# Loading and scanning the first 256 tokens whole instead of in two pieces, in a gated recurrence followed by a cosine feed-forward

## The chip, the cores and the metric

The kernel runs on one core of one Trainium2 chip. The metric is the device time of one execution in microseconds (us). One execution was also profiled, and its trace is what the lines below come from; a trace's span is about 1.8 us shorter than the time of the same execution. All executions quoted here were fast. A single core has no second die to compare with, so "fast" says only that the execution was within 1.5% of the fastest.

## The reference

```python
def _attn_ref(x, f_logit, lower_bound):          # x: 4 x 6080 x 256
    sig = 1.0 / (1.0 + np.exp(-f_logit))
    f = lower_bound + (1.0 - lower_bound) * sig
    i = 1.0 - f
    for t in range(S):
        h = f[:, t] * h + i[:, t] * x[:, t]
        y[:, t] = h
    return y

def _moe_ref(x, w_in, w_out):                    # w_in 256 x 2048, w_out 2048 x 256
    h = x @ w_in
    g = h * np.cos(h)
    return g @ w_out
```

The recurrence's output is the feed-forward's input. All is float32 outside; the kernel multiplies in float16.

## The kernel before

Tokens go through in chunks: seven of 256, then 512 each. For a chunk, ScalarE makes the gate, VectorE or GpSimd the term u, TensorE (chunks 0 to 3) or a transposing DMA (chunk 4 and later) turns both so that channels lie on partitions, VectorE scans, and the result yb feeds `mm1` (with w_in), a cosine, a product T, and `moe2` (with w_out). w_in comes in four quarters of its columns. Quarters 0 and 1 come as float32 ("raw") over SyncE's queue and are rounded by engines; quarters 2 and 3, all of w_out and the inputs of chunk 2 come over GpSimd's queue ("GpSimd's stream" below). `keep_warm` issues matmuls on zeros ("junk") that keep TensorE's clock up while it waits. The loads of chunk 3 and later wait until w_out's last quarter is in place.

```python
    emit_load(0, 0, P)                     # z and x of tokens 0..127
    load_win(0, cast=False)                # raw quarter 0, SyncE's queue
    emit_load(0, P, HALF)                  # tokens 128..255
    load_win(1, cast=False)
    emit_load(1)
    ...
    round_win(0, 0, nc.gpsimd.tensor_copy)
    load_win(2)                            # GpSimd's queue from here
    load_win(3)
    round_win(1, 0, nc.gpsimd.tensor_copy)
    load_wout(0); load_wout(1)
    emit_load(2, q=nc.gpsimd)
    load_wout(2)
    w_in_place = load_wout(3)              # chunk 3's loads wait for this one
    ...
    for c in range(3, NC):                 # woven between the matmul groups
        ...                                # chunk 4 on: less_one, pool_term (GpSimd),
        ...                                # turn (DMA transpose), forget (GpSimd), recur, cast
```

## Time and profile before

| | before |
|---|---|
| time, median of the three executions | 681.64 us (680.82 to 681.65) |
| TensorE busy | 670.9 of 679.7 us (99%) |
| VectorE, ScalarE, GpSimd busy | 583.2, 518.2, 315.1 us |
| TensorE's clock | 1.000 |

At a share of 99% the end moves when TensorE's few idle stretches move. They lie in the first 37 us of the trace ("the head"), with one of 0.35 us at 99 us. The profile's lines are shown in the prediction.

### The profile page before, as it was taken

To read this page: it belongs to the slowest core of one execution; us is meant where nothing else is said; L and a number is where in the kernel's file an instruction comes from. 1 tells how busy PE (TensorE), PEld (TensorE's weight loads), DVE (VectorE), ACT (ScalarE), POOL (GpSimd) and SP (SyncE) were. 2 spreads that over 40 slices of the span, in tenths; PEclk is the share of its full clock that TensorE was granted. 3 is DMA by queue.
4 is the path that set the end of the run, shared out by engine and by line. 5 is a ranking of instruction groups with operands and counts; after the bars stand their busy time and mean duration, and the time that the engine had idled before them with its cause. 6 is when DMAs were issued, how large, how long until landed. Compare 5 with 4: busy or idle time off the path is not lost.

```text
span 679.7 us, 12405 instructions
## 1 busy us (share of the span) xinstructions
PE 670.9 (99%) x4826; PEld 494.6 (73%) x4826; DVE 583.2 (86%) x507; ACT 518.2 (76%) x587; POOL 315.1 (46%) x442
## 2 busy tenths in 40 slices
PE   7999999999999999999999999999999999999998
PEld 4899987777777777777777777777777777777776
DVE  5898998888888888888888888888888888888884
ACT  6887788777877788777877788777877788777762
POOL 5478454445454445445454445445454445445300
DMA  8799756656667556764776556764686566632301
GB/s 205 198 259 225 201 157 154 169 140 124 160 188 150 124 140 175 167 139 125 159 189 150 124 142 175 158 148 124 163 185 149 124 144 178 162 76 63 94 32 62
DMA packets 173290, 101.99 MB, mean 150 GB/s; under 512 B 99120, under 2 KB 172080, under 8 KB 173232
## 3 DMA queue, kind: packets, MB, share of 16 engines
q1 hardware_dynamic: 171680, 99.11, 59.5%
q0 software_dynamic: 1280, 2.10, 1.7%
q8 instruction: 37, 0.61, 0.4%
q14 instruction: 21, 0.17, 0.1%
q10 hardware_dynamic: 272, 0.00, 0.0%
HBM read 54.00 MB, written 24.90 MB: 116 GB/s over the span
## 4 chain that ended last, share of the span: by engine, by line
PE 88%; DVE 4%; DMA 3%; issue 2%; ACT 1%; POOL 1%; SPq 0%; ACTq 0%; DVEq 0%; POOLq 0%
PE pb L312 45%; PE pa L271 43%; DVE T L286 3%; DVE ya L218 2%; DMA wo<-in_moe_w_out_dram 1%; DMA wir<-in_moe_w_in_dram 1%; ACT cs L280 1%; DMA zt<-in_f_logit_dram 1%; ACT ig L122 0%; SPq L82 0%; POOL wo L106 0%; POOL u L163 0%; ACT ig L150 0%; POOL xt L82 0%; POOL zt L82 0%
## 5 line engine op out<-in xcount | busy, mean ns | idle before, releaser
L286 DVE TENSOR_TENSOR T<-pa,cs 128x1024 f16<-128x1024 f32 x380 | 449.1, 1212 | 81.5 <-ACT cs L280 81.1
L280 ACT ACTIVATE cs<-pa 128x1024 f32<-128x1024 f32 x380 | 389.3, 1028 | 144.0 <-PE pa L271 132.4
L312 PE MATMUL pb<-wo,T 128*128 128x256 f16 x3040 | 393.0, 273 | 0.6 <-DMA wo<-in_moe_w_out_dram 0.6
L271 PE MATMUL pa<-yb,wi 128*128 128x512 f16 (+2 forms) x1736 | 390.3, 353 | 2.9 <-DMA wi<-in_moe_w_in_dram 1.4
L312 PEld LDWEIGHTS <-T 128*128 128x128 f16 x3040 | 297.3, 98 | 100.1 <-issue 1.0
L271 PEld LDWEIGHTS <-wi 128*128 128x128 f16 x1736 | 193.3, 114 | 75.5 <-issue 2.0
L232 POOL TENSOR_SCALAR yb<-ya,hc 128x512 f16<-128x512 f32 (+1 forms) x97 | 65.8, 679 | 187.5 <-DVE ya L218 186.6
L218 DVE TENSOR_TENSOR_SCAN ya<-ff,ya,ut 128x512 f32<-128x512 f32 (+4 forms) x94 | 131.3, 1398 | 0.6 <-POOL ff L199 0.6
L163 POOL TENSOR_TENSOR u<-ig,xt 128x256 f16<-128x256 f32 x182 | 130.3, 748 | 0.0
L161 POOL CAST ih<-ig 128x1024 f16<-128x1024 f32 (+1 forms) x47 | 47.5, 1010 | 137.1 <-ACT ig L150 135.1
L199 POOL TENSOR_SCALAR ff<-it,hp 128x512 f32<-128x512 f16 (+1 forms) x94 | 62.9, 683 | 1.5 <-DMA it<-ih 1.5
L320 ACT COPY osb<-pb 128x512 f32<-128x512 f32 x93 | 53.8, 579 | 0.7 <-PE pb L312 0.7
L122 ACT ACTIVATE ig<-zt 128x1024 f32<-128x1024 f32 (+2 forms) x52 | 51.7, 994 | 2.0 <-DMA zt<-in_f_logit_dram 1.9
L150 ACT ACTIVATE ig<-ig 128x1024 f32<-128x1024 f32 x44 | 46.9, 1066 | 0.0
L339 PE MATMUL warm<-junk 128*128 128x512 f16 x15 | 5.7, 543 | 1.3 <-POOL junk L328 1.3
L218 DVE TENSOR_TENSOR_SCAN ya<-ff,ya,tp 128x256 f32<-128x256 f32 (+1 forms) x8 | 5.0, 665 | 1.3 <-ACT ff L196 1.3
L218 DVE TENSOR_TENSOR_SCAN ya<-ff,ut 128x320 f32<-128x320 f32 (+2 forms) x6 | 5.6, 928 | 0.0
L317 DVE COPY osb<-pb 128x256 f32<-128x256 f32 x4 | 1.7, 424 | 4.5 <-PE pb L312 4.5
L139 DVE SCALAR_TENSOR_TENSOR u<-ig,xt 128x512 f16<-128x512 f32 (+1 forms) x5 | 3.2, 645 | 2.5 <-DMA xt<-in_x_dram 1.7
L339 PEld LDWEIGHTS <-junk 128*128 128x128 f16 x18 | 2.1, 126 | 4.0 <-issue 2.2
L137 POOL TENSOR_SCALAR ih<-ig 128x512 f16<-128x512 f32 x2 | 1.7, 866 | 6.2 <-ACT ig L122 6.2
L99 POOL CAST wi<-wir 128x512 f16<-128x512 f32 x2 | 1.5, 748 | 4.9 <-DMA wir<-in_moe_w_in_dram 4.8
(29 smaller groups left out, 27.2 us busy)
## 6 DMA issues: line engine op xcount, KB each, us to landing
zt<-in_f_logit_dram SPq DMA_DIRECT2D x44, 512.0 KB, 5.1
xt<-in_x_dram SPq DMA_DIRECT2D x44, 512.0 KB, 6.0
out_dram<-osb SPq DMA_DIRECT2D x43, 512.0 KB, 3.4
out_dram<-osb SPq DMA_DIRECT2D x7, 256.0 KB, 5.1
zt<-in_f_logit_dram SPq DMA_DIRECT2D x5, 256.0 KB, 5.2
xt<-in_x_dram SPq DMA_DIRECT2D x5, 256.0 KB, 5.6
wir<-in_moe_w_in_dram SPq DMA_DIRECT2D x2, 512.0 KB, 5.4
wo<-in_moe_w_out_dram POOLq DMA_DIRECT2D x4, 256.0 KB, 7.1
```

Source lines behind the costliest of these rows:

```text
L122: nc.scalar.activation(ig[:, ks, :], zt[:, ks, :], AFT.Tanh, bias=0.0, scale=0.5)
L150: nc.scalar.activation(ig[:, ks, :], ig[:, ks, :], AFT.Identity, bias=-1.0, scale=1.0)
L161: nc.gpsimd.tensor_copy(by_half(ih), split(ig))
L163: nc.gpsimd.tensor_tensor(by_half(u)[:, k], split(ig)[:, k], split(xt)[:, k], AOP.mult)
L199: nc.gpsimd.tensor_scalar(f[:, a:b], igt[:, i, 0:b - a], hp[:, i:i + 1], 1.0, AOP.mult, AOP.add)
L218: nc.vector.tensor_tensor_scan(ya[:, p:q], f[:, p:q], ut[:, i, p - a:q - a], init, AOP.mult, AOP.add)
L232: nc.gpsimd.tensor_scalar(yb[:, a:b], held[f"ya{i}", c][:, a:b], hc[:, i:i + 1], 0.0, AOP.mult, AOP.add)
L271: nc.tensor.matmul(pa[c, g][:, jq, a:b], win_block(i, jt), held[f"yb{i}", c][:, first + a:first + b], start=(i == 0), stop=(i == ND - 1))
L280: nc.scalar.activation(cs[c, g], pa[c, g], AFT.Sin, bias=float(_HALF_PI), scale=1.0)
L286: nc.vector.tensor_tensor(T, pa[c, g], cs[c, g], AOP.mult)
L312: nc.tensor.matmul(ps[:, ts % 2, :], Tt[c, ts, jt], wo[:, jt, :], start=(jt == 0), stop=(jt == NJ - 1))
L320: nc.scalar.copy(osb[:, ts - 1:ts + 1, :], ps)
```

## The change

Its intent: the first chunk of 256 tokens runs through in one go, with half as many instructions, and GpSimd is spared one rounding so that it issues its transfers sooner.

```diff
-    emit_load(0, 0, P)
+    emit_load(0)
     load_win(0, cast=False)
-    emit_load(0, P, HALF)       # it stood between raw quarters 0 and 1
 ...
     round_win(0, 0, nc.gpsimd.tensor_copy)
     load_win(2)
     load_win(3)
-    round_win(1, 0, nc.gpsimd.tensor_copy)
     load_wout(0)
 ...
-    gate(0, 0, P); term(0, 0, P); turn(0, 0, P)
-    keep_warm(8)
-    forget(0, 0, P); settle(0, 0, P)
-    gate(0, P, HALF)
-    round_win(0, 1, nc.vector.tensor_copy)
-    term(0, P, HALF); turn(0, P, HALF); forget(0, P, HALF)
-    mm1(0, 0, 0, P)
-    settle(0, P, HALF)
-    keep_warm(3, 1)
-    round_win(1, 1, nc.vector.tensor_copy)
-    mm1(0, 0, P, HALF)
+    gate(0); term(0); turn(0)
+    keep_warm(6)
+    forget(0)
+    round_win(0, 1, nc.scalar.copy)
+    settle(0)
+    round_win(1, 0, nc.vector.tensor_copy)
+    round_win(1, 1, nc.vector.tensor_copy)
+    mm1(0, 0)
```

(The `hc`, `hp` and lower-bound lines and the split of chunk 0's PSUM tile are left out.)

More of the change, by code (lines that the diff above doesn't have):

```diff
@@ L168, in turn @@
         if c < NPE:
-            apart = c == 1
+            apart = c < 2
             got = [ppool.tile([P, 1 if apart else 2, ND, HALF], f16, tag="p2", bufs=2,
@@ L328, with keep_warm @@
     nc.gpsimd.memset(junk, 0.0)
-    def keep_warm(k, g=None):
-        if g is None:
-            ps = ppool.tile([P, CH], f32, tag="p1", bufs=3, name=f"warm{len(warm)}",
-                            padded_shape=[P, 2 * CH])
-            warm.append(ps)
-        else:
-            ps = room(0, g)[:, 0:CH // HALF, :].rearrange("p j n -> p (j n)")
+    def keep_warm(k):
+        ps = ppool.tile([P, CH], f32, tag="p1", bufs=3, name=f"warm{len(warm)}",
+                        padded_shape=[P, 2 * CH])
+        warm.append(ps)
         for _ in range(k):
@@ L368 @@
     nc.vector.tensor_copy(ident, ident32)
-    gate(0, 0, P)
-    term(0, 0, P)
+    gate(0)
+    term(0)
     nc.vector.tensor_scalar(hc, lb, 0.5, -0.5, AOP.mult, AOP.add)
     nc.vector.tensor_scalar(hp, lb, -0.5, 0.5, AOP.mult, AOP.add)
-    turn(0, 0, P)
-    keep_warm(8)
-    forget(0, 0, P)
-    settle(0, 0, P)
-    gate(0, P, HALF)
-    round_win(0, 1, nc.vector.tensor_copy)
-    term(0, P, HALF)
-    turn(0, P, HALF)
-    forget(0, P, HALF)
-    mm1(0, 0, 0, P)
-    settle(0, P, HALF)
-    keep_warm(3, 1)
+    turn(0)
+    keep_warm(6)
[3 more added lines that the diff above has]
+    round_win(1, 0, nc.vector.tensor_copy)
     round_win(1, 1, nc.vector.tensor_copy)
-    mm1(0, 0, P, HALF)
+    mm1(0, 0)
     gate(1)
```

## The prediction

> **What bounds the kernel now.** I read the page's shares first, then busy time in stretches, then TensorE's instructions in the first 22 us, then the chain that ended last.
>
> The windows view gives busy time by stretch (columns: stretch, its length, then busy us and count for PE, PEld, DVE, ACT, POOL, then clock, DMA share, GB/s).
>
> ```profile
> 8.00:10.00 2.00, 1.43 (x15) 0.86 (x13) 1.12 (x4) 1.20 (x4) 1.92 (x4) 1.00 0.98 249
> 20.00:22.00 2.00, 1.75 (x17) 1.51 (x18) 1.84 (x3) 1.56 (x3) 0.00 (x0) 1.00 0.12 26
> 38.00:660.00 622.00, 621.62 (x4430) 455.65 (x4428) 545.82 (x459) 483.65 (x537) 295.45 (x406) 1.00 0.62 151
> ```
>
> From 38 to 660 us TensorE is busy 621.62 of 622 us, at full clock. The change touches only instructions issued before about 12 us. So it can move the end only by moving the moment at which TensorE becomes continuously fed. That moment is found in TensorE's timeline (start, duration, engine, line, operands, count; in brackets the idle time before and what ended it).
>
> ```profile
> 9.81 1.68 PE L271 MATMUL pa<-yb,wi 128*128 128x128 f16 x16 [0.57 <-ACT yb L225]
> 11.34 0.39 PE L176 MATMUL tp<-ident,ih 128*128 128x128 f16 x4
> ...
> 12.08 1.06 PE L271 MATMUL pa<-yb,wi 128*128 128x256 f16 x8
> 14.49 2.04 PE L271 MATMUL pa<-yb,wi 128*128 128x256 f16 x16 [1.35 <-DMA wi<-in_moe_w_in_dram]
> ...
> 17.36 0.60 PE L312 MATMUL pb<-wo,T 128*128 128x256 f16 x4 [0.38 <-DMA wo<-in_moe_w_out_dram]
> ...
> 21.08 0.60 PE L312 MATMUL pb<-wo,T 128*128 128x256 f16 x4 [0.25 <-DMA wo<-in_moe_w_out_dram]
> ```
>
> The first chunk's own work (row at 9.81) is not the last limit. After it TensorE waits four times for weights: the trace has quarter 2 of w_in landing at 12.03 (row at 12.08), quarter 3 at 14.45, quarter 1 of w_out at 17.32 and quarter 3 of w_out at 21.04. After 21.08 it has one more gap, 0.48 us at 36.97. The chain of waits says where that one comes from (start, length, what):
>
> ```profile
> 3.11 5.97 DMA wir<-in_moe_w_in_dram
> 9.08 0.06 issue
> 9.14 0.61 POOL wi L99
> 9.75 1.29 POOL wo L106 x2
> 11.04 0.71 POOL zt L82
> 11.76 0.73 POOL xt L82
> 12.49 0.55 POOL wo L106
> 13.04 8.00 DMA wo<-in_moe_w_out_dram
> 21.04 0.02 issue
> 21.06 0.37 SPq L82
> ```
>
> Inputs of chunks 3 to 6 are held back until the last w_out quarter has landed (21.04), and the gap at 37 hangs on these inputs. Both late limits therefore start from one time, the landing of w_out's last quarter. At first sight the chain promises a gain: its second step is GpSimd waiting for raw quarter 1 and rounding it (0.61 us), which the change deletes. But its 8.00 us step is a queueing time. GpSimd issued that last transfer by 13.62, and the transfers landing in front of it came at 16.01, 17.32, 18.04, 18.75 and 19.79. From 10 to 20 us the windows give DMA shares of 1.10, 0.91, 1.08, 1.08 and 0.99. The 16 engines are full, so an earlier issue only makes the transfer wait longer. What counts is when this stream starts: its first packet is at about 9.0 us.
>
> **What the Trainium skill says.** "DMA: Bandwidth & Descriptors", section "Issuing engines are not separate DMA queues", says that transfers of all issuing engines end on the same 16 DMA engines and interleave. The trace agrees: packets of SyncE's and GpSimd's queues overlap between 9 and 10 us at a share of 0.98. "SBUF — State Buffer", section "Who interferes with whom", says that a two-port VectorE operation, copies and casts among them, and GpSimd lock each other out of a shared port pair. The trace fits: GpSimd's 128x512 cast took 0.89 us beside VectorE's cast at 6.58 and 0.61 us at 9.14 with no such cast beside it. "TensorE: Matmul & The Clock Gate", section "What's actually happening", says that about 3.4 us of activity releases a halved clock. The 128x512 warming matmuls start 427 ns apart up to 5.56 us and 216 ns apart from 5.96, which agrees.
>
> **The change, part by part.**
>
> Loads. z and x of chunk 0 become two 256 KB transfers instead of four of 128 KB. SyncE issues two fewer transfers, each about 0.48 us from one issue to the next, so quarter 1 is issued at about 2.13 instead of 3.11. Bytes are unchanged. What moves is the order: 256 KB of 1,024-byte packets now stand ahead of raw quarter 0. These packets took 46 ns each; 256 of them on 16 engines are 256 x 46 / 16 = 0.74 us. Quarter 0 was issued at 1.66 in both, so it lands about 0.65 us later, 6.53 to about 7.2 (I take off 0.1 because in the kernel before, pieces behind it already shared its tail). Quarter 1 has the same bytes ahead as before and lands at about 9.0 (9.08 before), at best a few tenths sooner.
>
> First scan. z lands at about 3.55. A tanh of 128x512 took 0.64 us (row of chunk 1), and the 1-tanh copy the same: ih is ready at 4.85. u (0.68 us) is ready at about 4.95, as x lands near 4.3. Eight transposes at 107 ns, still cold, end near 5.9, the first four near 5.45. Two forget factors at 0.42 us (0.84 for two, at 11.76) end at 6.5. Two scans at 0.69 us (1.38 for two, at 12.86) end near 7.4, and VectorE's yb near 7.7. ScalarE now rounds half of quarter 0 before its yb: 7.2 + 0.64 = 7.85, then yb 0.51 = 8.4. The first real matmul starts at about 8.4 against 7.99, but it is the whole chunk: eight steps of 109 ns end it at 9.3, where before its second half started at 9.81.
>
> Quarter 1. VectorE rounds both halves, 2 x 0.42 from 9.05: ready at 9.9, against 10.36. Its matmuls run from 9.9 to 10.8, against 10.4 to 11.5. The transposes of chunk 1 remain tied to u of chunk 1 near 11.6, since VectorE does 0.42 us more before it but starts the pair 0.9 us sooner. So TensorE is through with chunk 1's transposes at about 12.0 as before, and the 0.6 us won before that become waiting for quarter 2.
>
> GpSimd. It gains 0.61 us and its wait for quarter 1, but it starts 0.65 us later on quarter 0. Its cast is now beside ScalarE's and not VectorE's; I take 0.65 us instead of 0.89. So it starts issuing quarter 2 at 7.2 + 0.05 + 0.65 = 7.9 against 7.41, and the stream's first packet is at 9.0 + 0.45 = 9.45. By 9.0 SyncE's queue is nearly drained (62 packets of 1,024 bytes left, 0.18 us of 16 engines), so the delay mostly becomes idle DMA time. Of the 0.45 us I count 0.1 as returned, because in that stretch SyncE's packets have the engines alone. w_out's first transfer is then issued at about 7.9 + 1.65 = 9.55, close to the old 9.69 and far ahead of its turn.
>
> Sum: the last w_out quarter lands 0.35 us later, 21.4. Nothing after it absorbs this: TensorE's wait of 0.25 us becomes 0.6, and the loads that lead to the gap at 37 shift with it. 681.64 + 0.35 = 682.0; I add 0.1 for the lopsided risks below and predict 682.1.
>
> **The rivals.** (1) Quarter 0 lands no later, or GpSimd's issues decide. For it: the chain names GpSimd's second rounding. Against: the full DMA shares. Even if the landing came much sooner, TensorE's waits for weights after 14.49 are 0.38 + 0.25 = 0.63 us and other operands wait close behind; I would give this 681.2. (2) The slow start of w_in grows with the shift. Raw packets of 2,048 bytes took 185 to 257 ns at 3.5 to 4.5 us and 84 to 101 ns later; if that is a fixed time from first touch, quarter 0 slips the full 0.74, GpSimd's cast is again blocked (0.89), and the stream starts 0.8 us late: 682.4. (3) TensorE loses its clock. It has one pause more before the scans (4.3 to 5.0), two fewer warming matmuls then and three fewer later, and a wait from 10.8 to 11.2. At half clock the eight matmuls after quarter 2 cost 0.9 us more, but 1.35 us of waiting for quarter 3 covers them; only if it were still cold after 14.8 would up to some 1.5 us show: 683.5. I give this one in ten. (4) The early first matmul wins. It would need weights to be there; they are not, so its worth is zero.
>
> **Range and chances.** The three timed runs before span 680.82 to 681.65, a spread of 0.8 us, as large as the effect. With rivals at 681.2 and 682.4 and the rare 683.5, I take 681.2 to 683.0. A move of 2% is 13.6 us; the whole head up to 21 us has 21 us in it and neither version can gain or lose that much. Within 2%: 0.99.
>
> **What would show it.** Raw quarter 0 landing near 7.2; GpSimd's first issue near 7.9; first matmul near 8.4; quarter 2, 3 and last w_out landing each about 0.35 us later (12.4, 14.8, 21.4), with the wait before that last one grown to about 0.6. If w_out's last quarter lands at or before 21.0 while quarter 0 lands late, the argument that the stream's start decides is wrong. If matmuls after 12 us step by 213 ns, rival 3 is true.

## The result, and the profile after

The changed kernel took 683.51 us (683.28 to 683.55, four executions) beside 681.23 us (680.58 to 681.65) for the kernel before. The ratio is 1.0034, 95% interval 1.0016 to 1.0051. Ratios here are the mean time of one kernel's fast executions over that of the other's of the same rounds, so not quite the ratio of the medians that are quoted. The time lies outside the range of 681.2 to 683.0, though within 2% as forecast.

TensorE after, first 22 us (columns as in the prediction):

```profile
8.59 2.42 PE L271 MATMUL pa<-yb,wi 128*128 128x256 f16 x16 [1.30 <-ACT yb L225]
...
12.96 1.06 PE L271 MATMUL pa<-yb,wi 128*128 128x256 f16 x8 [0.82 <-DMA wi<-in_moe_w_in_dram]
14.84 3.41 PE L271 MATMUL pa<-yb,wi 128*128 128x256 f16 x16 [0.81 <-DMA wi<-in_moe_w_in_dram]
18.04 1.27 PE L312 MATMUL pb<-wo,T 128*128 128x256 f16 x8
```

The first real matmul came at 8.59, quarter 2's at 12.96 and quarter 3's at 14.84; 8.4, 12.4 and 14.8 were predicted. But the 16 matmuls at 14.84 took 3.41 us where before they took 2.04. The windows view tells why in its clock column (third from the right):

```profile
14.00:16.00 2.00, 1.19 (x8) 0.92 (x8) 2.00 (x3) 1.05 (x2) 0.48 (x1) 0.77 1.10 197
16.00:18.00 2.00, 2.00 (x11) 1.42 (x10) 0.65 (x2) 1.04 (x1) 0.00 (x0) 0.50 1.08 335
...
38.00:660.00 622.00, 620.36 (x4419) 453.33 (x4419) 544.44 (x458) 483.00 (x536) 295.73 (x407) 1.00 0.60 151
```

TensorE ran at half its clock from 15.1 to 18.5 us. That is the third rival, for which the prediction had 683.5 us, just what was measured, and it is tempting to stop here. Two readings say that the match is luck. Of the four executions two had a mean clock of 0.997 (this stretch) and two 1.000, and they took 683.51 and 683.55 against 683.51 and 683.28: the same. And the lateness of one and the same product T in the two traces does not stay where the slow clock put it:

| product T number | ends, before | ends, after | later by |
|---|---|---|---|
| 5th | 19.07 | 20.57 | 1.50 |
| 10th | 29.57 | 30.05 | 0.49 |
| 29th | 64.11 | 65.61 | 1.50 |
| last | 670.71 | 672.62 | 1.91 |

By 30 us TensorE had caught up to 0.49 us, since it no longer had to stand where it stood before. Then, near 61 us, 1.4 us were lost anew (TensorE's `moe2` matmuls are 0.49 us late at 60.4 us and 1.91 us late at 64.9 us), long after the last changed instruction. In the last windows line above TensorE's busy time is 620.36 instead of 621.62 of 622 us. Its timeline shows the place, before:

```profile
59.28 1.04 PE L312 MATMUL pb<-wo,T 128*128 128x256 f16 x8
60.15 1.23 PE L271 MATMUL pa<-yb,wi 128*128 128x256 f16 x8
```

and after:

```profile
59.77 1.04 PE L312 MATMUL pb<-wo,T 128*128 128x256 f16 x8
61.70 0.27 PE L271 MATMUL pa<-yb,wi 128*128 128x256 f16 x1 [0.90 <-POOL yb L232]
62.37 0.93 PE L271 MATMUL pa<-yb,wi 128*128 128x256 f16 x7 [0.40 <-POOL yb L232]
```

TensorE waits for GpSimd's yb of chunk 7. GpSimd's timeline before it, first in the kernel before:

```profile
51.18 0.93 POOL L232 TENSOR_SCALAR yb<-ya,hc 128x256 f16<-128x256 f32 x2
52.09 1.36 POOL L199 TENSOR_SCALAR ff<-it,hp 128x512 f32<-128x512 f16 x2
...
59.04 1.36 POOL L232 TENSOR_SCALAR yb<-ya,hc 128x512 f16<-128x512 f32 x2
```

and in the changed one:

```profile
51.79 0.93 POOL L232 TENSOR_SCALAR yb<-ya,hc 128x256 f16<-128x256 f32 x2
54.00 1.37 POOL L199 TENSOR_SCALAR ff<-it,hp 128x512 f32<-128x512 f16 x2 [1.28 <-DMA it<-ih]
...
60.96 1.36 POOL L232 TENSOR_SCALAR yb<-ya,hc 128x512 f16<-128x512 f32 x2
```

Before, GpSimd works from 45.7 to 60.4 us without a gap, and TensorE takes its last yb the moment it is ready: this feed had no slack that TensorE's busy share could show. After, GpSimd stands 1.28 us for the transpose of chunk 7. That transpose was issued 0.61 us later (48.29 against 47.68) but landed 2.07 us later (53.91 against 51.84). The trace records 16 completions of each such DMA, and the last of them is its landing: 51.69 to 51.84 for all 16 before; 52.53 to 52.62 for fifteen of them after, and 53.91 for the sixteenth.

What delayed one completion? The trace lists, beside data packets, packets of kind "instruction": blocks of 8 KB and 16 KB of the program itself, fetched while it runs. Before, 8 KB blocks were fetched at 42.7, 45.3 and 51.9 us; after, at 44.4, 52.05 and 52.94. One of these two now ends just before the first completion and the other begins between the fifteenth and the sixteenth. The transpose has 32 packets of 4 bytes, which I take for its completion packets; 30 start up to 52.098, and the last two at 52.359 and 52.365, just as the block begun at 52.053 ends at 52.362. From this I formed theory I: the change shortened VectorE's program by 6 instructions (621 to 615), so that its next block is fetched some 7 us later, amid this transpose, and holds a completion back. The Trainium skill's "DMA: Bandwidth & Descriptors", section "Queues, rings and completion order", says that a DMA engine alternates between its queues by packet, and that a completion is written only after every earlier write of that DMA engine, whatever its queue. That fits such a delay, but the trace doesn't name the DMA engine of a packet, so one trace can't show the link.

All 18 traces together can. Of their 1,692 DMA transposes 39 had a sixteenth completion over 0.5 us after the fifteenth (0.67 to 1.66 us). Near every one of the 39 (from 1 us before its first completion on) a block was fetched, and in 37 of them two 4-byte packets start, after a pause of 60 ns or more, within 20 ns of that block's end; in none of the other 1,653 do they. So such a block does hold completions back. It seldom does: 241 transposes had a block as near and no such delay. And it explains only part of the delay: above, the packets were held for 0.26 us and the sixteenth completion came 1.29 us late. Where the rest comes from stays open.

### The profile page after: what moved, and what is told of

Its sections match the earlier page's. It is cut to its first block, busy times and chain, and to the rows that moved or that the text cites. A ratio compares the mean times of both kernels' runs of the same rounds, so it can differ in the third digit from the quotient of the medians.

```text
span 681.7 us, 12365 instructions
## 1 busy us (share of the span) xinstructions
PE 671.0 (98%) x4813; PEld 492.9 (72%) x4813; DVE 582.5 (85%) x503; ACT 518.3 (76%) x583; POOL 313.8 (46%) x441
## 4 chain that ended last, share of the span: by engine, by line
PE 88%; DVE 4%; POOL 3%; DMA 3%; issue 2%; ACT 1%; SPq 0%; POOLq 0%; ACTq 0%
PE pb L312 44%; PE pa L271 43%; DVE T L286 2%; DVE ya L218 1%; POOL u L163 1%; DMA it<-ih 1%; DMA wi<-in_moe_w_in_dram 1%; DMA wir<-in_moe_w_in_dram 1%; ACT cs L280 1%; POOL yb L232 1%; POOL ff L199 1%; POOL ih L161 0%; ACT ig L122 0%; POOL ig L147 0%; PE tp L176 0%
## 5 line engine op out<-in xcount | busy, mean ns | idle before, releaser
L271 PE MATMUL pa<-yb,wi 128*128 128x512 f16 (+1 forms) x1728 | 391.7, 355 | 4.8 <-DMA wi<-in_moe_w_in_dram 1.6
L122 ACT ACTIVATE ig<-zt 128x1024 f32<-128x1024 f32 (+1 forms) x51 | 51.4, 1008 | 2.7 <-DMA zt<-in_f_logit_dram 2.7
L139 DVE SCALAR_TENSOR_TENSOR u<-ig,xt 128x512 f16<-128x512 f32 x4 | 2.7, 685 | 3.0 <-DMA xt<-in_x_dram 2.8
L218 DVE TENSOR_TENSOR_SCAN ya<-ff,ya,tp 128x256 f32<-128x256 f32 x6 | 4.1, 732 | 0.0
```

The lines of the kernel that those rows point to most:

```text
L122: nc.scalar.activation(ig[:, ks, :], zt[:, ks, :], AFT.Tanh, bias=0.0, scale=0.5)
L218: nc.vector.tensor_tensor_scan(ya[:, p:q], f[:, p:q], ut[:, i, p - a:q - a], init, AOP.mult, AOP.add)
L271: nc.tensor.matmul(pa[c, g][:, jq, a:b], win_block(i, jt), held[f"yb{i}", c][:, first + a:first + b], start=(i == 0), stop=(i == ND - 1))
```

## The experiments

The sets ran on three different chips (the first eight runs on one), each set with executions of the kernel before on its own chip. Those had medians of 680.76 to 681.13. Ratios below are against them. (On the first chip, nine of the ten executions that the second four runs are compared with are those of the first four runs' set.)

**again**: the changed kernel, no edit.

> The changed kernel once more, for a second trace and for the clock of each execution. Theory C (the halved TensorE clock from 15.1 to 18.5 us of the first trace is the loss): executions at mean clock 0.997 take about 683.5 us, executions at 1.000 about 681.3. Theory F (the loss of about 1.9 us is made near 60 us, in the feed chain of GpSimd and DMA transposes, where the 48.3 us transpose landed 2.07 us late and TensorE then stood 0.9 + 0.4 us; a small lateness at 37 us is enough to set it off): 683.3 to 683.6 whatever the clock, and TensorE gaps of over 0.3 us again between 55 and 70 us.

Measured: 683.08 us (682.76 to 683.60), ratio 1.0032. One execution had clock 0.997 and took 682.76, the fastest; four at 1.000 took 682.87 to 683.60. Theory C falls as the main cause. But this trace (a slow-clock one) had no gap near 60 us: the sixteenth completion came 0.17 us after the fifteenth, and its 1.17 us of lateness at the end all came from the head, with w_out's last quarter landing at 22.03. So one time has two different make-ups. Theory F's "whatever the clock" holds, with a median a little under its range; its gaps do not occur in each execution.

**a_alone**: the first chunk whole, rounding as before.

```diff
     load_win(3)
+    round_win(1, 0, nc.gpsimd.tensor_copy)
 ...
-    round_win(0, 1, nc.scalar.copy)
     settle(0)
-    round_win(1, 0, nc.vector.tensor_copy)
+    round_win(0, 1, nc.vector.tensor_copy)
```

> First chunk whole, but both w_in quarters rounded as before (GpSimd one half, VectorE the other). If the whole first chunk is the cause: about +2 us against the kernel before, as the full change. If the moved rounding is the cause: within 0.5 us of the kernel before.

Measured: 683.73 us, ratio 1.0041. The whole first chunk is the cause. At full clock in its trace, TensorE had gaps of 0.57 and 0.40 us at 61 us, and the sixteenth completion came 1.23 us after the fifteenth.

**b_alone**: the kernel before with quarter 1 rounded by VectorE alone.

```diff
-    round_win(1, 0, nc.gpsimd.tensor_copy)
 ...
+    round_win(1, 0, nc.vector.tensor_copy)
     round_win(1, 1, nc.vector.tensor_copy)
```

> The kernel before with only the second quarter's rounding moved to VectorE alone. The recorded prediction's reading (the DMA stream is full, an earlier issue of w_out buys nothing): within 0.4 us of the kernel before. If the moved rounding is the cause of the loss: about +2 us.

Measured: 681.08 us, ratio 1.0002 (0.9989 to 1.0014). The moved rounding is worth nothing either way, as predicted, though the chain of waits named it.

**warm**: the changed kernel with its clock kept.

```diff
+    keep_warm(4, 2)      # junk into the PSUM tile that quarter 2's matmuls write next
     moe1(0, 2)
+    keep_warm(3, 3)
     moe1(0, 3)
```

> The changed kernel with 4 junk matmuls ahead of the matmuls of quarter 2 and 3 ahead of those of quarter 3, where TensorE waits 0.8 us each for the weights, to keep its clock. Theory C: every execution at clock 1.000 and about 681.3 us. Theory F in its plain form: the clock is 1.000, the half-speed stretch is gone, and the time stays within 0.5 us of 683.5, since executions of the changed kernel at clock 1.000 took that long too.

Measured: 682.67 us (681.92 to 683.63), ratio 1.0029; every clock 0.999 or 1.000. The median lies 0.8 us under 683.5, where theory F allowed 0.5, but only 0.4 under run again of the same set. At most a few tenths of the loss are the clock's. Its trace is the plainest case for theory I: at the 10th product it was level with the kernel before (0.01 us ahead), the transpose near 48 us was issued at 47.72 against 47.68, and still its last completion came at 53.10 against 51.84, 1.03 us after the fifteenth. TensorE then stood 0.57 and 0.40 us, and the end was 1.07 us late.

**pad**: six tiny instructions give VectorE its old count.

```diff
     nc.gpsimd.memset(junk, 0.0)
+    for k in range(6):
+        nc.vector.memset(cpool.tile([P, 1], f32, name=f"pad{k}"), 0.0)
```

> The changed kernel with six memsets of 128x1 at the head of VectorE's program, which give it back the 6 instructions that the change took off that engine (621 before, 615 changed, 621 now). Theory I (the late transpose near 48 us is late because VectorE's next block of instructions, 8 KB, is now fetched at 52 to 53 us, amid the completion of that transpose, and not at 45 us as in the kernel before): the fetch returns to 45 to 47 us, the 16th completion of the transpose comes within 0.2 us of the 15th (1.0 to 1.3 us after it in three of the four traces with the whole first chunk), TensorE has no gap over 0.3 us from 55 to 65 us, and the time falls from +2.3 to about +1.1 us over the kernel before. Rival D (the DMA engines are simply overtaken by loads at that place, or the chain is late): nothing changes, +2.3 us.

Measured: 681.99 us (681.44 to 684.54), ratio 1.0014 (the rounds compared leave the 684.54 out; with it the plain means give 1.0022). One of the two blocks fetched near 52 to 53 us was now fetched at 48.35 us, and in run pad_warm at 46.05; six more instructions of VectorE moved it, so it is VectorE's. The sixteenth completion came 0.10 us after the fifteenth. The profiled execution was the outlier of 684.54: its clock was halved for 6.8 us in the head, it was 2.48 us behind the kernel before at the 10th product (in part because quarter 3 landed at 15.70 instead of 14.45), and one gap of 0.40 us stood at 63 us, where theory I expected none over 0.3. GpSimd no longer waits at the place in question:

```profile
54.11 0.93 POOL L232 TENSOR_SCALAR yb<-ya,hc 128x256 f16<-128x256 f32 x2
55.06 1.36 POOL L199 TENSOR_SCALAR ff<-it,hp 128x512 f32<-128x512 f16 x2
```

**pad_warm**: both edits.

> Both remedies: the six memsets, and the seven junk matmuls that kept the clock (run warm). Theory I plus a head that is 0 to 0.5 us late: +0.2 to +0.7 us over the kernel before. Rival D: about +1.9 us, as run warm alone.

Measured: 682.18 us (681.50 to 682.43), ratio 1.0016. The gaps near 60 us are gone (0.10 us left, completions 0.03 us apart). What remains, about 1.1 us in the means, is more than expected; with nothing lost near 61 us I put it down to the head.

**before_pad**: the control, the same six memsets in the kernel before.

> Control: the kernel before with the same six memsets. They run in VectorE's idle first 1.8 us. Both theories, if the memsets themselves are free and the earlier fetch (expected near 40 us) meets nothing: within 0.3 us of the kernel before. A clear loss would show that such a fetch can also hurt elsewhere.

Measured: 680.80 us, ratio 1.0003. The memsets are free. This trace shows that such late completions are not the change's alone: the transpose issued at 27.64 had its fifteenth completion at 30.38 and its sixteenth at 32.03, beside a 16 KB block fetched from 30.03 to 30.96, and nothing was waiting for it. Here TensorE, 1.18 us ahead of the first trace, waited 0.38 us for GpSimd's yb at 59.6 us without a late completion.

**early**: GpSimd issues quarter 2 before it waits for raw quarter 0.

```diff
-    round_win(0, 0, nc.gpsimd.tensor_copy)
     load_win(2)
+    round_win(0, 0, nc.gpsimd.tensor_copy)
     load_win(3)
```

> The changed kernel with quarter 2 of w_in issued by GpSimd before it waits for and rounds raw quarter 0. The recorded prediction's step (the head is late because this stream of GpSimd transfers starts late): its first packet comes near 2.5 us, the last w_out quarter lands at least 0.3 us before 21.2, and the head's loss shrinks by as much. Rival (all 16 engines are busy from 2 us on anyway, so an earlier start only delays raw quarter 0): w_out's last quarter lands no earlier than 21.0, the first real matmul comes about 0.7 us later than 8.6, and the time is the changed kernel's or worse.

Measured: 682.64 us, ratio 1.0023. The stream started at 5.83 (not 2.5), and w_out's last quarter landed at 19.52, 1.6 us sooner than in the first trace after. So the start of the stream does bear on that landing, though 3.9 us at the start became 1.6 us at the end. The time did not follow: raw quarter 1 now landed at 10.38, TensorE waited 1.34 us for it and ran at half its clock from 11.1 to 14.5 us, and gaps of 0.36 and 0.40 us stood near 61 us although the sixteenth completion came 0.06 us after the fifteenth. There TensorE was 0.15 us behind the kernel before, but GpSimd's chain had the transpose issued 0.90 us later (48.58). So the 60 us place can bind without a late completion, when GpSimd is later than TensorE.

**pad_act**: the control for pad.

```diff
     nc.scalar.preload_act_table_set("silu_and_others")
+    for k in range(6):
+        nc.scalar.copy(cpool.tile([P, 1], f32, name=f"pad{k}"), junk[:, 0:1])
```

> Control for run pad: six tiny 128x1 copies at the head of ScalarE's program instead of VectorE's, which stays at 615 instructions. Theory I: VectorE's fetch stays at 52 to 53 us, the time stays +1.9 to +2.4 us over the kernel before. If any six extra instructions helped (rival: mere chance of placement): about +1.1 us, as run pad.

Measured: 682.20 us (681.63 to 683.12), ratio 1.0011. A miss: it came out like pad. In its trace the two blocks stayed, at 51.34 and 51.87 us, as expected, but the sixteenth completion came only 0.18 us after the fifteenth. No run of the changed kernel was in this set.

**xlate**: raw quarter 0 ahead of x.

```diff
-    emit_load(0)                            # z, x
+    emit_load(0, part=slice(0, 1))          # z
     load_win(0, cast=False)
+    emit_load(0, part=slice(1, 2))          # x
     load_win(1, cast=False)
 ...
-    keep_warm(7)
+    keep_warm(17)                           # and pad's memsets
```

> The whole first chunk with run pad's memsets, but raw quarter 0 ahead of x of chunk 0 in SyncE's queue (z, raw quarter 0, x, raw quarter 1), so that 256 KB stand ahead of it as in the kernel before, and 10 more junk matmuls at the start to cover the later x. The recorded prediction's step (the 256 KB more ahead of raw quarter 0 delay GpSimd's stream and with it everything): raw quarter 0 lands at 6.2 to 6.7 us and not at 7.1 to 7.7, the last w_out quarter at 20.2 to 21.0 and not at 21.2 to 22.2, and the time falls from +1.2 (run pad) to +0.5 us or less, unless the first matmuls, now near 10.5 us, come to bind. Rival (the whole chunk costs by its own lateness, not through the stream): +1.2 us or more.

Measured: 681.47 us (681.00 to 681.66) beside 681.13, ratio 0.9998 (0.9984 to 1.0013). Raw quarter 0 landed at 6.18, the stream's first packet came at 8.48, w_out's last quarter landed at 20.36. GpSimd's timeline of xlate:

```profile
6.24 0.61 POOL L99 CAST wi<-wir 128x512 f16<-128x512 f32 x1 [4.47 <-DMA wir<-in_moe_w_in_dram]
6.79 1.64 POOL L93 DMA_DIRECT2D wi<-in_moe_w_in_dram  x2
```

The changed kernel has the same two rows at 7.54 and 8.10. The first real matmul came at 9.89, 1.3 us later than in the changed kernel, and it didn't matter. With both causes removed, no loss of the whole first chunk is resolved: it is 0.34 us by the medians and none by the means, for three executions of the kernel before on this chip took 682.27 to 683.59.

**stream**: pad_warm, with GpSimd freed of its rounding.

```diff
-    round_win(0, 0, nc.gpsimd.tensor_copy)
-    load_win(2)
+    # load_win(2) waits for the landing of raw quarter 0 alone
 ...
     settle(0)
+    round_win(0, 0, nc.vector.tensor_copy)
```

> Run pad_warm with GpSimd freed of its rounding: VectorE rounds both halves' share of it, and GpSimd issues quarter 2 as soon as raw quarter 0 has landed (about 7.4 instead of 7.8). Same step, other route: first packet of the stream 0.3 to 0.5 us earlier than in pad_warm (9.34), last w_out quarter as much earlier (21.44), time +0.7 to +0.9 us over the kernel before instead of +1.2. Rival (the stream's start does not decide): +1.2 us.

Measured: 681.49 us median (681.19 to 681.62, and one of 685.45), ratio 1.0009 (0.9987 to 1.0030). First packet at 8.93, w_out's last quarter at 21.12. By the median it is 0.36 us over the kernel before, less than the 0.7 to 0.9 expected; the outlier, at clock 0.997, makes the interval wide and I rest nothing on it.

**best**: the same freeing in the kernel before.

> The kernel before with the same freeing of GpSimd: quarter 2 issued at the landing of raw quarter 0 (about 6.4), VectorE rounding both halves. If the stream's start decides the head: stream 0.5 to 0.8 us earlier than 8.9, last w_out quarter near 19.9, time 0.3 to 0.7 us under the kernel before. Rival (TensorE's own first work binds next): no difference.

Measured: 681.05 us (680.22 to 681.38), ratio 0.9993 (0.9976 to 1.0009). The stream started at 8.46 and w_out's last quarter landed at 20.22. A gain is possible but not resolved. No version here is shown to beat the kernel before.

The next four ran as one set, because pad_act had left theory I open.

**again2**: the changed kernel, no edit.

> The changed kernel unaltered, on the chip of the next three. Both theories: +2 us or a little more over the kernel before. In its trace theory I expects VectorE's fetch within 1 us of the completions of the transpose near 48 us, and, in most executions, the 16th of them 1.0 to 1.3 us after the 15th with TensorE gaps of 0.9 to 1.3 us together near 61 us.

Measured: 683.13 us (682.18 to 684.30), mean 683.11, ratio 1.0029. At full clock, the two blocks were fetched at 51.07 and 51.60, the completions came from 51.55 to 51.65 and the last at 52.64. TensorE:

```profile
60.40 0.27 PE L271 MATMUL pa<-yb,wi 128*128 128x256 f16 x1 [0.42 <-POOL yb L232]
61.07 0.93 PE L271 MATMUL pa<-yb,wi 128*128 128x256 f16 x7 [0.40 <-POOL yb L232]
```

**pad2**:

> Run pad once more. Theory I: 0.9 to 1.3 us under run again2. If run pad's gain was the chip's or chance: equal to again2.

Measured: 682.36 us (681.29 to 682.94), mean 682.21, ratio 1.0015 (1.0003 to 1.0027), so 0.90 us under again2 in the means, as theory I expected. With five executions of each, spread over 1.7 and 2.1 us, this difference alone is not clear of noise. Completions 0.02 us apart, no gap of over 0.2 us near 60 us. Its trace's head was very late (w_out's last quarter at 22.70), and that alone made its execution slow (682.94).

**pad_act2**:

> Run pad_act once more. Theory I: equal to run again2 within 0.4 us. If any six instructions help: 0.9 to 1.3 us under again2, as pad2. A value between the two would say that the late completion is a matter of a few tenths of a microsecond of timing, which six copies on ScalarE shift too.

Measured: 682.89 us (681.26 to 684.23), ratio 1.0025, 0.21 us under again2 in the means, as theory I expects of it. In its trace the blocks were fetched at 53.39 and 54.06 and the last completion was 0.26 us late.

**xlate_nopad**: xlate without the memsets.

> Run xlate without the memsets, VectorE back at 615 instructions. Theory I: the fetch returns to 51 to 53 us, a late completion in its trace or in most executions, and 0.7 to 1.2 us more than xlate's 0.0 to +0.3 over the kernel before. If the fetch is harmless: equal to xlate.

Measured: 682.22 us (681.97 to 682.90), ratio 1.0017 (1.0004 to 1.0029). Blocks fetched at 51.51 and 52.07, fifteenth completion at 52.14, sixteenth at 53.12, TensorE gaps of 0.54 and 0.40 us near 61 us. With the head in time (raw quarter 0 at 6.14), it took 1.10 us more than the kernel before by the medians, where xlate took 0.34 more; by the ratios the six missing instructions cost 1.3 us.

All traces together, by VectorE's instruction count as built (the traces record two fewer of each), for the transpose issued near 48 us (last column: how long after the fifteenth completion the sixteenth came, in us):

| VectorE's program | traces | sixteenth completion later by |
|---|---|---|
| 615 instructions | after, a_alone, warm, again2, xlate_nopad | 1.29, 1.23, 1.03, 0.99, 0.98 |
| 615 instructions | again, pad_act, pad_act2, early | 0.17, 0.18, 0.26, 0.06 |
| 621 or more | before, b_alone, before_pad, best, pad, pad2, pad_warm, stream, xlate | 0.10 at most |

Five of nine against none of nine. In each of the five the last two completion packets start within 4 ns of the end of VectorE's block, 0.20 to 0.26 us after the rest; in none of the other traces do they. The block fetched amid the completions goes with the delay but doesn't force it: in pad and before_pad another 8 KB block was fetched amid them, and the sixteenth came 0.10 us after the fifteenth at most. Which executions it hits I can't tell, since the traces don't name a packet's DMA engine. Against the first trace of before, TensorE's `moe2` matmuls lost 0.95 to 1.43 us near 61 us in the five late traces, 0.89 us in early, and at most 0.50 us in the other twelve.

## Why the prediction was wrong

**"So it can move the end only by moving the moment at which TensorE becomes continuously fed."** This is the step that failed. From 38 to 660 us TensorE was busy 621.62 of 622 us, and I took that as proof that nothing there could go wrong. But a busy share tells nothing of the slack of what feeds it. GpSimd's chain from 45.7 to 60.4 us had none, and one DMA completion 1 to 1.3 us late went straight through it to the end. The change reached that place through instruction counts: 6 fewer instructions of VectorE moved the fetch of its next block from 45.3 us to 51 to 53 us. Runs pad2 against again2 (0.90 us in the means) and xlate_nopad against xlate (0.8 us by the medians, 1.3 by the ratios) put this part near 1 us; the traces, nine with the six instructions missing against nine with them, put it at 0.6 us in the mean (0.73 against 0.14 us lost near 61 us). None of my four rivals contained it. The intervals of single runs are about as wide (0.0012 to each side is 0.8 us), so the size is known roughly; that it exists rests on the traces above all.

**The head's mechanism was right, its size was not.** The 256 KB ahead of raw quarter 0 delay GpSimd's stream and with it w_out's last quarter; xlate, which took them away, lost the head's loss. The traces agree: over the ten with no late completion near 48 us (without early, and without pad and pad_act2 with their halved stretch of 6.8 us), w_out's last quarter landed between 20.15 and 22.70 us, and the last product ended between 0.90 us sooner and 1.34 us later than in the first trace, in nearly the same order. But the term was mis-sized. Three traces of the kernel before and its near copies (before, b_alone, before_pad) against ten with the whole first chunk and the changed load order (without xlate, xlate_nopad, early and stream), means:

| | before | whole chunk | later by | predicted |
|---|---|---|---|---|
| raw quarter 0 lands | 6.39 | 7.41 | 1.02 | 0.65 |
| first packet of GpSimd's stream | 8.93 | 9.65 | 0.72 | 0.45 |
| quarter 3 lands | 14.06 | 15.19 | 1.13 | 0.35 |
| last quarter of w_out lands | 20.54 | 21.66 | 1.12 | 0.35 |

In the means of these traces the first packet of raw quarter 0 already started 1.05 us later (3.87 against 2.82). Its issue was 0.09 us later (1.75 against 1.66), and the packets of z and x ahead of it took 1.69 us of 16 engines where half as many took 0.83, so the 256 KB more cost 0.86 us and not 0.74. The 0.1 us that I took off for pieces sharing its tail was not there. (GpSimd's start, 7.9 against 7.41, is also 0.49 us later, not the 0.45 that I carried on.) And nothing was "returned" between the first packet and the landing: another 0.4 us was added by quarter 3's landing. The sign that I named, TensorE's wait before w_out's last quarter grown to 0.6 us, did not come: in the traces at full clock that still have this wait it is 0.24 to 0.38 us (a_alone, warm, pad_warm, again2), since TensorE is late already by quarters 2 and 3. Rival 2 (682.4, stream 0.8 us late) was nearer in size, but its blocked cast was not seen: GpSimd's took 0.61 us in the first trace after. The head's loss is 1.0 to 1.1 us (pad, pad2, pad_warm: ratios 1.0014 to 1.0016, each uncertain by some 0.8 us), three times my 0.35. The two parts sum to 1.7 to 2.1 us; 2.0 to 2.3 were measured.

**One trace of before was too little.** Its execution took 681.46 us, 0.7 above the 680.76 us that was the median beside b_alone, and its last w_out quarter landed at 21.04 where the near copies have 20.15 and 20.43. Compared with the first trace after (21.16) the head seems to have lost only 0.12 us, which would have confirmed a small shift. Ten traces show 1.12.

**The early stream start** (rival 1 and the chain's GpSimd row): rightly given no worth; b_alone measured 1.0002.

**The clock** (rival 3) was given one chance in ten and appeared in 2 of the first 4 executions, but its price was misjudged in kind. In the first four executions those at full clock took as long as those with the halved stretch (683.51 and 683.28 beside 683.51 and 683.55), and in run again the halved one was the fastest. With again2 five halved ones have a mean of 683.46 us and nine at full clock 683.08, which is within noise. Of the lateness after a halved stretch of 3.4 us about 1 us is caught up by 30 us, for TensorE then doesn't stand where it otherwise waits for w_out (no such wait in the first trace after, 0.40 and 0.26 us in pad_warm). Of the longer stretches of 6.8 us little is caught up by then (pad 684.54 us, pad_act2 683.75). The Trainium skill's "TensorE: Matmul & The Clock Gate", section "What's actually happening", gives a window of about 3.4 us for the gate, and the trace's 3.41 us agrees. (The release at the start, for which the prediction quoted it, agrees loosely: matmuls ran from 1.31 us and the step fell to 216 ns at 5.96.)

**The early first matmul** was given no worth; xlate, with its first matmul at 9.89 instead of 8.59, took 0.9998 of the time before (0.9984 to 1.0013). Nothing speaks against it.

## What to carry to other kernels

A saturated engine's busy share says nothing of the slack of its feeders: before trusting it, look for a stretch where another engine on the feeding chain works without a gap and ends just as it is needed. Order the first loads by which one starts the longest stream behind it, not by which data are used first. When a change of the head costs more than the head shows, compare the same instruction of both traces along the whole run, take several traces of each kernel, and look at what the program's own length moves.

## What the Trainium skill lacked or had wrong

- "Runtime: NRT & Kernel Launch", section "Instruction fetch mechanics", says that instructions are refilled in 16 KiB blocks and that crossing a block is mostly hidden. The traces show 37 blocks of 16 KB and 21 of 8 KB in a run. Their cost to other transfers is on no page: next to a block, 39 of 1,692 transposes had a completion 0.67 to 1.66 us late. Six tiny VectorE instructions moved one 8 KB fetch from 51 to 53 us back to 45 to 48 us, and with it went completions of 0.98 to 1.29 us delay. "DMA: Bandwidth & Descriptors", section "Queues, rings and completion order", lists queue row 14 as runtime-internal (refill among its uses) and could name this cost; the traces show the 8 KB blocks on a queue numbered 14 and the 16 KB ones on 8.
- The same section says that a completion waits for every earlier write of its DMA engine, but gives no size: here one of 16 completions came up to 1.29 us after the fifteenth beside an 8 KB block, and in one trace 1.65 us (30.38 to 32.03) beside a 16 KB block.
- "DMA: Bandwidth & Descriptors", section "Issuing engines are not separate DMA queues", has starting transfers on several engines save only issue time, and says nothing of what a later start of one of them does to its end. Here the 16 engines were full for most of the head, and a first packet 0.72 us later went with an end of the stream 1.12 us later.
- "TensorE: Matmul & The Clock Gate" agrees with the traces: half clock for 3.41 us, twice that (6.83 us) in two traces.
